# Moving the minimum-and-add of the Q features from VectorE to GpSimd in a linear-attention and MLP block

## Chip, cores and metric

The kernel runs on one core of a Trainium2 chip. The metric is the device time of one execution in microseconds (us). Medians and ratios here are of fast runs, or of samples in which a rare slow run does not move the median.

## The reference

Two branches share one layer-normalised input `xn` of 2048 tokens by 640 features, and their sum is added to `x`. The branch that matters here is linear attention with 32 heads of 20 features:

```python
qkv = (x @ wqkv) ...                                  # q, k, v
phi = lambda t: jnp.where(t > 0, t + 1, jnp.exp(t)) + 1e-6
pq, pk = phi(q), phi(k)
kv  = einsum("bhsd,bhse->bhde", pk, v);  z = einsum("bhsd->bhd", pk)
num = einsum("bhqd,bhde->bhqe", pq, kv)
den = einsum("bhqd,bhd->bhq", pq, z)[..., None] + 1e-6
o   = num / den  ...  @ wo
# result: x + attention(xn) + (gelu(xn @ w1 + b1) @ w2 + b2)
```

Inputs and outputs are bf16.

## The kernel before

The feature map `phi` is computed as `max(t, 0) + (min(exp(t), 1) + 1e-6)` in three instructions on two engines. ScalarE takes the exponential out of PSUM (where this kernel's matmuls put their results) into one of three buffers `ek` in SBUF (where its other tiles lie), VectorE applies minimum and add in place, and VectorE adds the maximum, again out of PSUM. Code and edits are shown cut in this document (`...`), and remarks after # are added here:

```python
def phi(src, b, nb, dst, res_dst, extra_w):           # v = "vector"
    s = ring_e[0] % 3                                  # one of three ek buffers
    ...
    Pl.ins("scalar", lambda e: e.activation(e2, src, ACT.Exp), reads=br, writes=[r_ek[s]])
    Pl.ins(v, lambda e: e.tensor_scalar(et, et, 1.0, 1e-6, ALU.min, ALU.add),
           reads=[r_ek[s]], writes=[r_ek[s]])
    Pl.ins(v, lambda e: e.scalar_tensor_tensor(out=d2, in0=src, scalar=0.0, in1=e2,
                                               op0=ALU.max, op1=ALU.add),
           reads=br + [r_ek[s]], writes=[res_dst] + extra_w)
```

The Q stage has four chunks of 512 tokens. Each chunk has five units of five 128x512 matmuls, one PSUM bank per unit, and a `phi` per unit. Between the chunks stand two other small stages:

```python
def q_chunk(c):
    for j in range(DT):                                # five units
        b = take(1)                                    # next of 8 PSUM banks, in a ring
        ...                                            # five matmuls into bank b
        phi(bank(b), b, 1, PQ[:, j, cc], r_PQ[c][j], [])

q_chunk(0)
kvt_step()        # five masked products, VectorE takes them out of PSUM
q_chunk(1)
q_chunk(2)
m_step()          # KV times Wo: five pairs of banks, ScalarE takes them out
q_chunk(3)
...
bs = [out_w2(0)]  # 24 matmuls of the MLP's second layer
db = den_step()   # denominators: needs every unit of Q
```

In these traces an engine takes up its work in program order: in the changed kernel, for example, TensorE's units of chunk 3 start at 139.67 us, behind the KV-Wo pairs that had to wait. A wait on a semaphore therefore holds everything behind it on the same engine, and the ring of eight banks lets TensorE run ahead only until it meets a bank that has not been emptied.

## Time and profile before

The median was 210.53 us (three runs, 210.5 to 210.66). The profiled execution has a span of 208.6 us.

| Reading | Value | View |
|---|---|---|
| TensorE busy | 98% of the span | busy table |
| VectorE, ScalarE, GpSimd busy | 52%, 36%, 11% | busy table |
| One Q unit on TensorE | about 1.09 us | timeline |
| Min/add, max/add of a Q unit on VectorE | 0.29, 0.69 us | timeline |
| Pause of TensorE's weight loads in the KV-Wo step | 0.42 us | timeline |

The page of before. Its busy table gives, for each engine, busy us, share of the span and number of instructions (PE is TensorE's matmuls, PEld its weight loads, DVE VectorE, ACT ScalarE, POOL GpSimd):

```profile
PE 204.4 (98%) x1599; PEld 140.6 (67%) x1599; DVE 108.1 (52%) x226; ACT 74.9 (36%) x142; POOL 22.9 (11%) x62
...
PE 92%; DVE 4%; DMA 3%; issue 0%; ACTq 0%; DVEq 0%
```

The last line is from the same page's chain of waits: the chain that ended last, followed back from the end, by engine. TensorE makes up 92% of it.

The timeline of before, from the first weight load of Q over the end of chunk 2 to the first of the denominators, gives start, length, engine, line, operation and tiles; brackets name what ended an idle time. L463 is the exponential, L464 the min/add, L466 the max/add, L551 the KV-Wo step, L526 the Q units and L561 the denominators:

```profile
104.12 5.22 PEld L526 LDWEIGHTS ps<-xnT,Wqkv 128*128 128x128 bf16 x25
...
121.12 0.60 ACT L463 ACTIVATE ek<-ps 128x512 bf16<-128x512 f32 x1 [0.48 <-PE ps L526]
121.75 0.30 DVE L464 TENSOR_SCALAR ek<-ek 128x512 bf16<-128x512 bf16 x1
122.10 1.52 PEld L551 LDWEIGHTS ps<-Wo,W 128*32 128x32 bf16 x48 [0.40 <-issue]
...
122.15 0.69 DVE L466 SCALAR_TENSOR_TENSOR PQ<-ps,ek 128x512 bf16<-128x512 f32 x1
122.20 0.60 ACT L463 ACTIVATE ek<-ps 128x512 bf16<-128x512 f32 x1 [0.48 <-PE ps L526]
122.83 0.29 DVE L464 TENSOR_SCALAR ek<-ek 128x512 bf16<-128x512 bf16 x1
...
123.23 0.69 DVE L466 SCALAR_TENSOR_TENSOR PQ<-ps,ek 128x512 bf16<-128x512 f32 x1
124.04 1.01 PEld L551 LDWEIGHTS ps<-Wo,W 128*32 128x32 bf16 x32 [0.42 <-ACT Msb L556]
...
134.07 0.77 PEld L561 LDWEIGHTS ps<-PQ,ZB 128*32 128x32 bf16 x20 [0.26 <-issue]
```

Two things are to be seen. Each min/add starts 0.03 us after its exponential ends, so VectorE, which is fully occupied here (0.29 + 0.69 us and two gaps in 1.08 us), is not behind. And the weight loads pause 0.42 us after 48 of 80, until the max/add of the last unit of chunk 2 has emptied its bank at 123.92. The bracket puts this down to ScalarE; the max/add's end, 0.12 us before the loads resume, and the chain of waits name the true releaser.

The trace has no large two-operation arithmetic on GpSimd. What it does have, by groups of one shape (busy us, then mean ns of one), is this:

```profile
L314 POOL TENSOR_SCALAR stats<-stats 128x1 f32<-128x1 f32 x16 | 3.5, 222 | 7.2 <-DVE stats L311 7.2
...
L277 POOL TENSOR_SCALAR_AFFINE_SELECT E<-E 128x512 bf16<-128x512 bf16 x1 | 0.6, 634 | 0.1
```

### The profile page before, as it was taken

Reading aid. Unit: us, or ns where it says so; the run is one execution under the profiler, and the core shown is the slowest. Engines: PE = TensorE matmul, PEld = TensorE weight load, DVE = VectorE, ACT = ScalarE, POOL = GpSimd, SP = SyncE. Lnnn points to the kernel's source line nnn. Section 1 sums busy time; section 2 is a strip of 40 time slices with the busy share of each in tenths; the row PEclk is TensorE's granted clock in tenths of the full one; section 3 lists DMA queues with packets and bytes.
Section 4 is the critical chain, followed back from the end, with each engine's and each line's share of the span. In section 5 each row is a group of like instructions: output and inputs, shape, how many; then the busy total and the mean of one; then the engine's idle time right before and its main releaser. Section 6 shows DMA issues by size and latency. Waiting matters only on the chain.

```text
span 208.6 us, 3973 instructions
## 1 busy us (share of the span) xinstructions
PE 204.4 (98%) x1599; PEld 140.6 (67%) x1599; DVE 108.1 (52%) x226; ACT 74.9 (36%) x142; POOL 22.9 (11%) x62
## 2 busy tenths in 40 slices
PE   7999999999999999999999999999999999999995
PEld 2789987444457777777756565577777777777775
DVE  4589970000007888998258965478633422523322
ACT  2689887666676455111153577100000000000000
POOL 3235568300031000000000000000000000000000
PEclk9999999999999999999999999999999999999999
DMA  5998668998000000000000000691110111001001
GB/s 172 348 351 103 104 127 120 376 332 274 3 0 0 0 3 0 0 3 0 0 3 2 0 3 0 198 312 54 63 60 31 61 42 52 31 31 35 31 35 61
DMA packets 22507, 17.86 MB, mean 86 GB/s; under 512 B 9176, under 2 KB 22488, under 8 KB 22488
## 3 DMA queue, kind: packets, MB, share of 16 engines
q1 hardware_dynamic: 21808, 17.11, 28.6%
q10 hardware_dynamic: 680, 0.49, 0.8%
q8 instruction: 12, 0.20, 0.4%
q14 instruction: 7, 0.06, 0.1%
HBM read 12.62 MB, written 2.62 MB: 73 GB/s over the span
## 4 chain that ended last, share of the span: by engine, by line
PE 92%; DVE 4%; DMA 3%; issue 0%; ACTq 0%; DVEq 0%
PE ps L622 33%; PE ps L355 25%; PE ps L514 10%; PE ps L476 10%; PE ps L526 7%; DVE PQ L466 3%; DMA W<-in_B_w_dram 3%; PE ps L658 2%; DVE ek L464 1%; PE ps L535 1%; PE ps L551 1%; PE ps L561 1%; PE ps L385 0%; PE ps L339 0%; ACTq L234 0%
## 5 line engine op out<-in xcount | busy, mean ns | idle before, releaser
L355 PE MATMUL ps<-xnT,W 128*128 128x128 bf16 (+2 forms) x435 | 52.0, 282 | 0.0
L622 PE MATMUL ps<-W,HG 128*128 128x320 bf16 x360 | 51.4, 299 | 0.0
L355 PEld LDWEIGHTS ps<-xnT,W 128*128 128x128 bf16 x435 | 35.5, 98 | 15.8 <-DMA W<-in_B_w_dram 0.2
L622 PEld LDWEIGHTS ps<-W,HG 128*128 128x128 bf16 x360 | 35.1, 98 | 14.2 <-issue 0.4
L359 ACT ACTIVATE HG<-ps,b1c 128x128 bf16<-128x128 f32 (+2 forms) x87 | 40.0, 492 | 12.7 <-PE ps L355 10.6
L464 DVE TENSOR_SCALAR ek<-ek 128x512 bf16<-128x512 bf16 (+1 forms) x36 | 11.1, 307 | 41.7 <-ACT ek L463 40.5
L641 DVE TENSOR_TENSOR out_sb<-ps,xnT 128x640 bf16<-128x640 f32 x15 | 12.4, 825 | 36.2 <-PE ps L622 36.0
L463 ACT ACTIVATE ek<-ps 128x512 bf16<-128x512 f32 (+1 forms) x36 | 23.2, 644 | 19.7 <-PE ps L526 10.1
L622 PE MATMUL ps<-Msb,PQ 128*128 128x320 bf16 x150 | 22.5, 299 | 0.0
L526 PE MATMUL ps<-xnT,Wqkv 128*128 128x512 bf16 x100 | 22.1, 379 | 0.0
L514 PE MATMUL ps<-xPK,xn_tm 128*128 128x320 bf16 x160 | 22.1, 299 | 0.0
L476 PE MATMUL ps<-Wqkv,xnT 128*128 128x320 bf16 x160 | 21.9, 299 | 0.0
L476 PEld LDWEIGHTS ps<-Wqkv,xnT 128*128 128x128 bf16 x160 | 15.7, 98 | 6.2
L514 PEld LDWEIGHTS ps<-xPK,xn_tm 128*128 128x128 bf16 x160 | 15.6, 98 | 6.0
L622 PEld LDWEIGHTS ps<-Msb,PQ 128*128 128x128 bf16 x150 | 14.6, 98 | 5.7
L526 PEld LDWEIGHTS ps<-xnT,Wqkv 128*128 128x128 bf16 x100 | 11.6, 118 | 9.5 <-ACT Msb L556 0.2
L311 DVE BATCH_NORM_STATS2 stats<-xPK 128x6 f32<-128x320 bf16 x32 | 13.6, 466 | 2.9 <-DMA xPK<-in_A_x_dram 2.7
L466 DVE SCALAR_TENSOR_TENSOR PQ<-ps,ek 128x512 bf16<-128x512 f32 x20 | 13.8, 692 | 2.1
L466 DVE SCALAR_TENSOR_TENSOR xPK<-ps,ek 128x640 bf16<-128x640 f32 x16 | 13.2, 825 | 1.7
L501 DVE TENSOR_TENSOR Msb<-Msb,xPK 128x640 f32<-128x640 f32 x14 | 11.6, 825 | 0.5
L518 ACT ACTIVATE W<-ps 128x640 bf16<-128x640 f32 x5 | 3.5, 703 | 18.6 <-PE ps L514 18.6
L321 POOL TENSOR_TENSOR rstd<-aggr,mhalf 128x1 f32<-128x1 f32 x16 | 9.1, 568 | 8.9 <-DVE aggr L319 8.9
(68 smaller groups left out, 93.9 us busy)
## 6 DMA issues: line engine op xcount, KB each, us to landing
xnT<-in_A_x_dram SPq DMA_DIRECT2D x4, 640.0 KB, 6.4
Wqkv<-in_A_wqkv_dram SPq DMA_DIRECT2D x3, 800.0 KB, 7.0
out_dram<-out_sb SPq DMA_DIRECT2D x15, 160.0 KB, 1.8
W<-in_B_w_dram SPq DMA_DIRECT2D x1, 1920.0 KB, 15.2
W<-in_B_w_dram SPq DMA_DIRECT2D x3, 480.0 KB, 7.4
xPK<-in_A_x_dram SPq DMA_DIRECT2D x2, 640.0 KB, 8.5
Wo<-in_A_wo_dram SPq DMA_DIRECT2D x1, 800.0 KB, 10.7
xPK<-in_A_x_dram SPq DMA_DIRECT2D x4, 160.0 KB, 4.4
```

What stands on the lines that cost most here:

```text
L311: Pl.ins(v, lambda e: e.bn_stats(stats[:, s, 6 * h:6 * h + 6], x_in[:, t, h * HW:(h + 1) * HW]), reads=[r_x[t]], writes=[r_stats[s][h]])
L355: Pl.ins("tensor", [(lambda e, k=k: e.matmul(bank(b, 0, w), W1[:, k, jb * P:(jb + 1) * P], xnT[:, k, tok], start=(k == 0), stop=(k == DT - ...
L359: Pl.ins("scalar", lambda e: e.activation(HG[:, jb, tok], bank(b, 0, w), ACT.Gelu_apprx_tanh, bias=b1c[:, jb:jb + 1]), reads=[B_[b], r_b1c ...
L463: Pl.ins("scalar", lambda e: e.activation(e2, src, ACT.Exp), reads=br, writes=[r_ek[s]])
L464: Pl.ins(v, lambda e: e.tensor_scalar(et, et, 1.0, 1e-6, ALU.min, ALU.add), reads=[r_ek[s]], writes=[r_ek[s]])
L466: Pl.ins(v, lambda e: e.scalar_tensor_tensor(out=d2, in0=src, scalar=0.0, in1=e2, op0=ALU.max, op1=ALU.add), reads=br + [r_ek[s]], writes= ...
L476: fns.append(lambda e, k=k, h=h, b=b, t=t: e.matmul(bank(b + h, 0, HW), xnT[:, k, t * P:(t + 1) * P], Wqkv[:, k, D + h * HW:D + (h + 1) * ...
L501: Pl.ins(v, lambda e, t=t: e.tensor_tensor(out=zsum, in0=zsum, in1=PK[:, t, :], op=ALU.add), reads=[r_PK[t], r_zsum], writes=[r_zsum])
L514: Pl.ins("tensor", [(lambda e, t=t, h=h, b=b, f=f: e.matmul(bank(b + h, 0, HW), xn_tm[:, t, f * P:(f + 1) * P], PK[:, t, h * HW:(h + 1) * ...
L526: Pl.ins("tensor", [(lambda e, k=k, j=j, b=b: e.matmul(bank(b), Wqkv[:, k, j:D:DT], xnT[:, k, cc], start=(k == 0), stop=(k == DT - 1))) fo ...
L622: return lambda e: e.matmul(bank(b + h, 0, HW), l, r[:, h * HW:(h + 1) * HW], start=(i == 0), stop=(i == JT + DT - 1))
L641: Pl.ins(v, lambda e: e.tensor_tensor(out=halves(out_sb[:, s, :]), in0=pair(b), in1=halves(x_res[:, t, :]), op=ALU.add), reads=B_[b:b + 2] ...
```

## The change

VectorE is the busier of the two engines and GpSimd is idle in the Q stage, so the change gives GpSimd the min/add of the twenty Q units. The K stage keeps VectorE.

```diff
-        def phi(src, b, nb, dst, res_dst, extra_w):
+        def phi(src, b, nb, dst, res_dst, extra_w, mid="vector"):
 ...
-            Pl.ins(v, lambda e: e.tensor_scalar(et, et, 1.0, 1e-6, ALU.min, ALU.add),
+            Pl.ins(mid, lambda e: e.tensor_scalar(et, et, 1.0, 1e-6, ALU.min, ALU.add),
 ...
-                phi(bank(b), b, 1, PQ[:, j, cc], r_PQ[c][j], [])
+                phi(bank(b), b, 1, PQ[:, j, cc], r_PQ[c][j], [], g)
```

## The prediction

> **What bounds the kernel now.** TensorE. The page's busy table gives PE 98% of the 208.6 us span, VectorE 52%, ScalarE 36%, GpSimd 11%. In the Q stage (104.3 to 130.9 us in the timeline) one unit of five 128x512 matmuls takes about 1.09 us. Per unit ScalarE's exponential takes 0.60 us, VectorE's min/add 0.29 us and its max/add out of PSUM 0.69 us; with the gaps VectorE repeats every 1.08 us. The chain of waits runs through these two VectorE lines from 115.7 to 123.9 us (3.7% of the span), but that mostly shows two engines with the same period: there the timeline has PE busy without a gap, and each min/add starts 0.03 us after its exponential, so VectorE has no backlog. PE's only real stall is in the step after chunk 2 (KV times Wo): its fourth output pair needs the PSUM banks of the last two Q units of chunk 2, and the weight loads pause 0.42 us (123.62 to 124.04) for the max/add that ends at 123.92.
>
> **What the change removes, adds, moves.** Twenty min/adds of 0.29 us (plus about 0.1 us gap each) leave VectorE. GpSimd, idle in this stage, gets twenty 128x512 bf16 one-input operations. The trace has no such GpSimd operation. Estimate: its affine selects take 0.34 us for 140 columns and 0.634 us for 512, so 0.79 ns per column over a fixed 0.23 us; its 128x1 add takes 0.22 us. That gives 0.65 us; a slower two-operation body could make it 0.9. The Trainium skill, "GPSIMD Engine Reference", section 4.1, calls one-input elementwise work on GpSimd roughly line-rate, which agrees with the affine selects. The trace shows about 0.08 us from VectorE to GpSimd and 0.14 us back.
>
> Contention: the max/add has one SBUF input (the other is PSUM), and the skill's "SBUF — State Buffer", section "Who interferes with whom", says such an instruction does not contend with GpSimd.
>
> **On the critical path.** The throughput gain is worth nothing: PE sets the 1.09 us. GpSimd keeps up while one operation with its gap stays under 1.08 us. The three exponential buffers need a latency of under three periods, about 3.2 us; the new one is about 2.2 us. What remains is latency: a unit's banks come free later by (0.65 + 0.2) minus (0.29 + 0.1), 0.4 to 0.7 us. This lands once in full, at the fourth pair of the KV-Wo step: the stall goes from 0.42 to about 0.9 us. The denominator step also waits for the last Q unit, but with about 1.3 us of slack (max/add ends 132.6, step starts 134.07).
>
> **Prediction.** 210.5 + 0.5 = 211.0 us, 80% range 210.6 to 213.0. Faster by over 2%: 0.01; within 2%: 0.90; slower by over 2%: 0.09.
>
> **What would show it.** GpSimd min/add 0.6 to 0.95 us; VectorE busy down by about 6 us, GpSimd up by 13 to 19 us; PE busy unchanged; the pause of weight loads at the fourth pair 0.8 to 1.1 us; no pause before the denominator step; max/add still 0.69 us.
>
> **What would make it wrong.** If the GpSimd operation takes over about 1.0 us, it sets the pace: units fall behind by the excess, times ten over chunks 1 and 2, plus five in chunk 3. At 1.35 us per unit that is 2.7 us plus added latency at the KV-Wo step, plus about 1 us at the denominator step: over 4 us, slower by over 2%.

## The result

The changed kernel took 231.66 us (median of four runs, 231.0 to 232.78) against 210.51 us of before on the same chip. The ratio is 1.1014, with a 95% interval of 1.0983 to 1.1046. Here and below, a ratio is the mean time of one kernel's fast runs over the mean of the other's of the same rounds, so it is not quite the ratio of the medians quoted.

The span grew from 208.6 to 229.3 us. The page of after: busy table, chain of waits by engine, and the two groups of the changed pair (count, busy us, mean ns, and idle time before them with its releaser):

```profile
PE 210.0 (92%) x1592; PEld 141.7 (62%) x1599; DVE 102.8 (45%) x206; ACT 75.0 (33%) x142; POOL 61.4 (27%) x82
...
PE 77%; POOL 14%; DVE 2%; issue 2%; DMA 1%; POOLq 1%; ACT 1%; SPq 0%; DVEq 0%; ACTq 0%
...
L464 POOL TENSOR_SCALAR ek<-ek 128x512 bf16<-128x512 bf16 x20 | 38.4, 1921 | 50.4 <-ACT ek L463 49.0
...
L466 DVE SCALAR_TENSOR_TENSOR PQ<-ps,ek 128x512 bf16<-128x512 f32 x20 | 13.8, 691 | 35.8 <-POOL ek L464 35.8
```

GpSimd, which was not in the chain before, now makes up 14% of it. The min/add takes 1.92 us on GpSimd, where the prediction had 0.65. The max/add is unchanged at 0.69 us, but now waits 35.8 us in total for GpSimd.

The timeline of after (cut):

```profile
104.00 5.22 PEld L526 LDWEIGHTS ps<-xnT,Wqkv 128*128 128x128 bf16 x25
...
106.10 29.94 POOL L464 TENSOR_SCALAR ek<-ek 128x512 bf16<-128x512 bf16 x15 [42.73 <-ACT ek L463]
...
125.73 0.75 PE L551 MATMUL ps<-Wo,W 128*32 128x320 bf16 x16
...
128.99 1.27 PE L551 MATMUL ps<-Wo,W 128*32 128x320 bf16 x16 [2.51 <-DVE PQ L466]
...
132.99 1.27 PE L551 MATMUL ps<-Wo,W 128*32 128x320 bf16 x16 [2.73 <-ACT Msb L556]
...
136.98 2.33 PE L551 MATMUL ps<-Wo,W 128*32 128x320 bf16 x32 [2.73 <-DVE PQ L466]
...
142.29 9.91 POOL L464 TENSOR_SCALAR ek<-ek 128x512 bf16<-128x512 bf16 x5 [6.25 <-ACT ek L463]
...
153.22 0.17 PEld L561 LDWEIGHTS ps<-PQ,ZB 128*32 128x32 bf16 x8 [3.80 <-DVE PQ L466]
153.26 2.33 PE L561 MATMUL ps<-PQ,ZB 128*32 128x512 bf16 x20 [3.49 <-DVE PQ L466]
```

GpSimd works through the fifteen units of chunks 0 to 2 back to back, 29.94 us for fifteen starts, or 2.0 us each. Then it has a hole of 6.25 us: the KV-Wo pairs wait for the last banks of chunk 2, and the units of chunk 3 stand behind those pairs in TensorE's queue. Then come the last five units, and the denominators (L561) start.

From the first weight load of Q to the first of the denominators it took 49.2 us (104.00 to 153.22) in place of 29.95 (104.12 to 134.07). The 49.2 us add up as 2.1 until GpSimd's first start, 29.9 for fifteen units, 6.25 of hole, 9.9 for five units, and 1.0 for the last max/add and its release. That is 19.3 of the 20.7 us by which the span grew; the denominators themselves took 1.07 us longer (2.33 against 1.26).

That last figure is a second effect. By stretches, the windows view gives length, busy us of PE, PEld, DVE, ACT and POOL, then the granted clock (1.00 is full speed), the DMA share and GB/s:

```profile
112.97:125.70 12.73, 10.97 (x49) 5.64 (x50) 5.50 (x11) 4.18 (x7) 12.25 (x7) 1.00 0.00 1
125.70:139.20 13.50, 5.54 (x81) 2.85 (x80) 4.15 (x6) 4.50 (x7) 9.95 (x6) 0.62 0.00 1
139.20:145.00 5.80, 5.45 (x22) 2.47 (x20) 0.68 (x1) 2.50 (x4) 2.63 (x2) 0.70 0.00 0
```

In the gaps of the KV-Wo step the granted clock falls. A pair that took 0.75 us at 125.73 takes 1.27 us from 128.99 on. In before, the same view gives 1.00 from 104.1 to 134.07.

### The profile page after: what moved, and what is told of

It reads as the page before. It is cut to its first block, busy times and chain, and to the rows that moved or that the text cites. A ratio compares the mean times of both kernels' runs of the same rounds, so it can differ in the third digit from the quotient of the medians.

```text
span 229.3 us, 3965 instructions
## 1 busy us (share of the span) xinstructions
PE 210.0 (92%) x1592; PEld 141.7 (62%) x1599; DVE 102.8 (45%) x206; ACT 75.0 (33%) x142; POOL 61.4 (27%) x82
## 4 chain that ended last, share of the span: by engine, by line
PE 77%; POOL 14%; DVE 2%; issue 2%; DMA 1%; POOLq 1%; ACT 1%; SPq 0%; DVEq 0%; ACTq 0%
PE ps L622 29%; PE ps L355 22%; POOL ek L464 14%; PE ps L514 9%; PE ps L476 9%; PE ps L658 2%; DMA xPK<-in_A_x_dram 1%; PE ps L526 1%; DVE PQ L466 1%; PE ps L551 1%; PE ps L561 1%; POOLq L692 1%; ACT ek L463 1%; DVE W L539 1%; PE ps L385 0%
## 5 line engine op out<-in xcount | busy, mean ns | idle before, releaser
L464 POOL TENSOR_SCALAR ek<-ek 128x512 bf16<-128x512 bf16 x20 | 38.4, 1921 | 50.4 <-ACT ek L463 49.0
L466 DVE SCALAR_TENSOR_TENSOR PQ<-ps,ek 128x512 bf16<-128x512 f32 x20 | 13.8, 691 | 35.8 <-POOL ek L464 35.8
L526 PE MATMUL ps<-xnT,Wqkv 128*128 128x512 bf16 x97 | 23.3, 397 | 3.7 <-DVE PQ L466 1.8
L464 DVE TENSOR_SCALAR ek<-ek 128x640 bf16<-128x640 bf16 x16 | 5.2, 324 | 33.8 <-ACT ek L463 32.6
L551 PE MATMUL ps<-Wo,W 128*32 128x320 bf16 x80 | 5.6, 436 | 8.0 <-DVE PQ L466 5.2
```

The lines of the kernel that those rows point to most:

```text
L464: Pl.ins(mid, lambda e: e.tensor_scalar(et, et, 1.0, 1e-6, ALU.min, ALU.add), reads=[r_ek[s]], writes=[r_ek[s]])
L526: Pl.ins("tensor", [(lambda e, k=k, j=j, b=b: e.matmul(bank(b), Wqkv[:, k, j:D:DT], xnT[:, k, cc], start=(k == 0), stop=(k == DT - 1))) fo ...
```

## The experiments

Theory A: GpSimd needs about 1.9 us for this operation by itself, more than TensorE's 1.09 us per unit, and so sets the pace. Its rivals: B, something beside it in the Q stage stretches a 0.65 us operation; C, three buffers are too few for the longer chain; D, the extra engine in the chain costs by itself.

### e1_bench: the operation alone

Added to the kernel before, on memory that is dead by then; fourteen forms, twice each, in this manner (each wait of GpSimd on itself is kept):

```diff
+            # sc, sd: 128x512 bf16; sf: fp32; started by the denominators
+            rep(lambda e: e.tensor_scalar(sc, sc, 1.0, 1e-6, ALU.min, ALU.add), R, W)
+            rep(lambda e: e.tensor_single_scalar(sc, sc, 1.0, ALU.min), R, W)
+            rep(lambda e: e.tensor_scalar(sc, sc, 1.0, 1e-6, ALU.mult, ALU.add), R, W)
+            ...
```

> The kernel before, with 28 GpSimd instructions (14 forms, twice each) on dead scratch memory, started when the denominators are done, so nothing waits for them and VectorE is mostly idle beside them. Theory A (GpSimd itself needs 1.92 us for this operation): the min/add on 128x512 bf16 takes about 1.9 us here too, about half at 256 columns and a quarter at 128 (plus a fixed part near 0.2 us), while the affine select stays near 0.63 us. Theory B (something in the Q stage, such as VectorE or ScalarE beside it, stretches a 0.65 us operation): it takes 0.65 to 0.9 us here. The one-operation forms tell what in it is slow: if each of the two operations costs a pass, min alone and add alone take about half, 0.9 to 1.1 us; if min is the slow one, add alone is near 0.65 and min alone near 1.9. If conversion from and to bf16 is what costs, the fp32 form is clearly faster.

Measured (one look, correct, 210.6 us). The per-line view of e1_bench gives minimum/median/maximum ns. L681 to L683 are the min/add at 512, 256 and 128 columns; L684 and L685 are minimum and add alone; L687 is multiply/add, L688 minimum/maximum; L689 is the min/add in fp32; L692 is a copy, L694 the affine select:

```profile
L681 POOL TENSOR_SCALAR xn_tm<-xn_tm x2: 1953/1975/1997, 141.0 to 143.1; 128x512 bf16<-128x512 bf16 x2
L682 POOL TENSOR_SCALAR xn_tm<-xn_tm x2: 1191/1218/1244, 145.2 to 146.4; 128x256 bf16<-128x256 bf16 x2
L683 POOL TENSOR_SCALAR xn_tm<-xn_tm x2: 681/778/876, 147.8 to 148.7; 128x128 bf16<-128x128 bf16 x2
L684 POOL TENSOR_SCALAR xn_tm<-xn_tm x2: 1487/1510/1533, 149.5 to 151.1; 128x512 bf16<-128x512 bf16 x2
L685 POOL TENSOR_SCALAR xn_tm<-xn_tm x2: 1490/1492/1495, 152.7 to 154.2; 128x512 bf16<-128x512 bf16 x2
...
L687 POOL TENSOR_SCALAR xn_tm<-xn_tm x2: 620/620/621, 159.0 to 159.7; 128x512 bf16<-128x512 bf16 x2
L688 POOL TENSOR_SCALAR xn_tm<-xn_tm x2: 614/614/614, 160.4 to 161.1; 128x512 bf16<-128x512 bf16 x2
L689 POOL TENSOR_SCALAR xn_tm<-xn_tm x2: 1985/2025/2065, 161.8 to 163.8; 128x512 f32<-128x512 f32 x2
...
L692 POOL COPY xn_tm<-xn_tm x2: 611/611/611, 173.2 to 173.9; 128x512 bf16<-128x512 bf16 x2
...
L694 POOL TENSOR_SCALAR_AFFINE_SELECT xn_tm<-xn_tm x2: 614/614/615, 177.2 to 177.8; 128x512 bf16<-128x512 bf16 x2
```

Theory A holds and B falls: the min/add takes 1.95 to 2.0 us here too, and 1.92 when written to another tile. The spans of GpSimd in a profile are rough, but the starts bear them out: those of the two min/adds lie 2.03 us apart, those of the two minimum/maximums 0.69. None of the three guesses about the cause was right. Minimum alone, add alone and multiply alone take about 1.5 us each, so it is neither the minimum nor one pass per operation; fp32 is no faster, so it is not the conversion. Two pairs, multiply/add and minimum/maximum, run at the speed of a copy, three times faster than the min/add and even 2.4 times faster than one of their own operations alone.

The run also shows GpSimd slowing VectorE, but only at times. VectorE's addition of two SBUF tiles (x plus bias) took 0.48 to 0.49 us in all 16 executions of before. Of the ten beside this measurement, three took 0.89 to 1.10 us and the other seven 0.48, among them three (at 151.89, 156.51 and 170.36 us) that lie wholly inside a GpSimd instruction which reads SBUF.

### e2_ring8: more buffers

```diff
             et = ek[:, s, 0:w]
+            r_e = r_ek[s]
+            if nb == 1:                        # Q units: eight buffers in dead memory
+                s = 4 + ring_q[0] % 8
+                ring_q[0] += 1
+                et, r_e = xn_tm[:, s, 0:w], r_xn[s]
 ...
```

> The changed kernel with eight exponential buffers in the Q stage in place of three. Theory A (GpSimd's throughput sets the pace): GpSimd still starts one min/add every 2.0 us, ScalarE merely runs further ahead, and the time stays within 1.5 us of 231.7. Theory C (the longer chain of exponential, min/add and max/add, held by three buffers, sets the pace): the units come every 1.1 to 1.3 us and the time falls to 211 to 215.

Measured: 231.63 us median of four runs, ratio 1.0998 (1.0945 to 1.1052). GpSimd still takes 1.92 us per unit and starts every 2.0 us; only the exponentials run further ahead. C falls. The page of e2_ring8 (L469 is the min/add, its buffers now in the tile `xn_tm`):

```profile
L469 POOL TENSOR_SCALAR xn_tm<-xn_tm 128x512 bf16<-128x512 bf16 x20 | 38.4, 1922 | 50.4 <-ACT xn_tm L468 49.0
```

### e3_short_op: the same chain with a short operation

```diff
-            Pl.ins(mid, lambda e: e.tensor_scalar(et, et, 1.0, 1e-6, ALU.min, ALU.add),
+            # on GpSimd only: passes everything, wrong result on purpose
+            Pl.ins(mid, (lambda e: e.tensor_scalar(et, et, 1.0, 1e-6, ALU.min, ALU.add)) if mid == "vector" else
+                   (lambda e: e.affine_select(out=et, in_=et, compare_op=ALU.is_ge, fill=0.0,
+                                              base=0, pattern=[[1, w]], channel_multiplier=0)),
```

> The changed kernel with GpSimd's min/add replaced by an affine select that passes every element (a wrong result on purpose: no minimum and no 1e-6). Same engines, same waits, same tiles, only the duration differs: 0.63 us as measured in the mask stage. Theory A: the whole loss is the duration; the time is what the prediction gave for 0.65 us, 210.8 to 211.3, and the pause of weight loads at the fourth pair of the KV-Wo step is 0.8 to 1.1 us. Rival D (the extra engine in the chain costs by itself, through its waits and hops): the time stays above 213.

Measured: 210.61 us median of six runs, before 210.28; ratio 1.0010 (0.9976 to 1.0043); the result is wrong as intended. The timeline of e3_short_op (L465 is the affine select, L553 the KV-Wo step):

```profile
122.70 0.61 POOL L465 TENSOR_SCALAR_AFFINE_SELECT ek<-ek 128x512 bf16<-128x512 bf16 x1 [0.47 <-ACT ek L463]
...
124.23 1.01 PEld L553 LDWEIGHTS ps<-Wo,W 128*32 128x32 bf16 x32 [0.78 <-ACT Msb L558]
```

All of the loss is the operation's duration; the added engine costs a pause that grows from 0.42 to 0.78 us. D falls, apart from those 0.36 us, which the time itself, with its interval of plus or minus 0.3%, doesn't resolve. The time fell just short of the 210.8 us that was expected as a minimum.

### e4_warm: keeping TensorE busy in its gaps

```diff
+        def fill(b, n):
+            Pl.ins("tensor", [lambda e: e.matmul(bank(b), warm[:, 0:P], warm[:], start=True, stop=True)] * n,
+                   reads=[r_warm], writes=[B_[b]])
 ...
+                if j > 0:
+                    fill(b, 8)           # before the last four pairs of the KV-Wo step
 ...
+            fill(b, 14)                  # before the denominators
```

> The changed kernel with dummy matmuls in the gaps of TensorE: eight of 512 columns before each of the last four pairs of the KV-Wo step and fourteen before the denominator step, in banks that are already free. The trace after shows a granted clock of 0.62 to 0.70 between 125.7 and 145 us and steps that took about twice as long as before (KV-Wo pairs four and five 2.33 against 1.2 us, first Q unit of chunk 3 1.93 against 1.05, denominators 2.33 against 1.26). If that slow clock is a part of the loss of its own, the clock stays near 1.0 in these stretches and the time falls by 2 to 3 us to about 229. If the clock is only a side effect hidden behind GpSimd, the time stays at 231.7 within 0.7.

Measured: 229.43 us median of four runs (229.35 to 229.57), ratio 1.0903 (1.0851 to 1.0955), against 1.1014 for after. The clock of the three stretches from 125.7 to 155 us is 1.00 throughout. In the timeline of e4_warm the pairs are back at their old length:

```profile
127.02 1.89 PE L544 MATMUL ps<-warm 128*128 128x512 bf16 x8 [0.51 <-DVE PQ L466]
129.02 0.75 PE L555 MATMUL ps<-Wo,W 128*32 128x320 bf16 x16
...
153.06 1.26 PE L568 MATMUL ps<-PQ,ZB 128*32 128x512 bf16 x20 [0.98 <-DVE PQ L466]
```

So some 2.2 us of the loss (231.66 to 229.43; the ratios, each to before on the same chip, differ by 1.1%, or 2.3 us) come from the slowed clock, shown by an edit that changes only what TensorE does in its gaps. By the two profiles hardly any of it was lost in the KV-Wo step itself, where GpSimd sets the pace: the denominators start only 0.2 us earlier (153.06 in place of 153.26), while they themselves are 1.07 us shorter. The page "TensorE: Matmul & The Clock Gate" of the Trainium skill, section "What's actually happening", says that a clock gate halves TensorE's rate when it has been idle. The trace of after agrees: from 129.0 to 130.3 us the granted clock was 0.51, and the pair's 0.75 us became 1.27. The page gives an idle window of about 3.4 us; here the pair at 128.99 ran slowly after a gap between matmuls of 2.51 us. But the length of one gap doesn't decide it: in e5_inter_after (below) a pair kept its 0.75 us after a gap of 2.38, and the ten matmuls after a gap of 1.25 ran slowly (3.63 us in place of 2.35). What decides it, no run here separates.

### e8_bench2: which pairs are quick

This continues the first measurement with other pairs, in the same manner.

> More forms of the operation alone on GpSimd, in the kernel before, as in the first measurement, where minimum with maximum and multiply with add took 0.61 to 0.62 us and minimum with add 1.92, and a minimum, add or multiply alone 1.5. Theory E: a few pairs have a quick routine of their own and all others take a general one. Then each pair falls into one of two groups, near 0.6 or near 1.9 us, and not in between. Rival F: the second operation decides, an add being slow after a minimum because of its kind (minimum and maximum are alike, multiply and add are alike, a mixed pair is slow); then maximum with minimum, add with multiply, add with add and multiply with multiply are all quick, and every mixed pair is slow.

Measured (one look, correct, 212.19 us). By the per-line view of e8_bench2, L681 is add/multiply, L682 multiply/multiply, L683 add/add, L684 maximum/minimum:

```profile
L681 POOL TENSOR_SCALAR xn_tm<-xn_tm x2: 620/642/665, 140.9 to 141.6; 128x512 bf16<-128x512 bf16 x2
L682 POOL TENSOR_SCALAR xn_tm<-xn_tm x2: 664/668/671, 142.4 to 143.1; 128x512 bf16<-128x512 bf16 x2
L683 POOL TENSOR_SCALAR xn_tm<-xn_tm x2: 1937/1966/1995, 143.9 to 146.0; 128x512 bf16<-128x512 bf16 x2
L684 POOL TENSOR_SCALAR xn_tm<-xn_tm x2: 2049/2104/2160, 148.0 to 150.1; 128x512 bf16<-128x512 bf16 x2
```

Maximum/add, add/maximum, multiply/minimum, minimum/multiply, minimum/minimum and subtract/multiply are slow as well (1.92 to 1.97 us). There are two groups and nothing between, as theory E has it. Rival F falls: add/add and maximum/minimum are slow although their operations are alike, and the order matters (minimum/maximum 0.61 us, maximum/minimum at least 2.05). Why these pairs are quick is not shown; that they have a routine of their own is a guess that fits.

### e6_minmax: the change with a quick pair, correct

Because the exponential is positive, a maximum with 0 changes nothing. The 1e-6 moves into VectorE's next instruction: `max(t, 1e-6) + min(exp(t), 1)` differs from `phi` by at most 1e-6.

```diff
-            Pl.ins(mid, lambda e: e.tensor_scalar(et, et, 1.0, 1e-6, ALU.min, ALU.add),
+            lim, op, low = (1e-6, ALU.add, 0.0) if mid == v else (0.0, ALU.max, 1e-6)
+            Pl.ins(mid, lambda e: e.tensor_scalar(et, et, 1.0, lim, ALU.min, op),
 ...
-            Pl.ins(v, lambda e: e.scalar_tensor_tensor(out=d2, in0=src, scalar=0.0, in1=e2,
+            Pl.ins(v, lambda e: e.scalar_tensor_tensor(out=d2, in0=src, scalar=low, in1=e2,
```

> The changed kernel with a correct result, but the second operation on GpSimd is a maximum with 0 in place of the addition of 1e-6, and the 1e-6 moves into VectorE's next instruction as the floor of its maximum. The measurement of forms gave 0.61 us for a minimum with a maximum, 1.92 for a minimum with an addition. If only the form of GpSimd's operation matters, the time is that of the affine select, 210.4 to 211.0 beside 210.3 of before on the same chip (ratio 1.000 to 1.003), with GpSimd's operation at 0.60 to 0.64 us.

Measured: correct, 210.75 us median of five runs, before 210.35; ratio 1.0014 (0.9982 to 1.0045). The per-line view of e6_minmax for the min/max (L465), and its timeline at the KV-Wo step (L552), one fence each:

```profile
L465 POOL TENSOR_SCALAR ek<-ek x20: 612/612/614, 106.0 to 131.8; 128x512 bf16<-128x512 bf16 x20
```

```profile
124.21 1.00 PEld L552 LDWEIGHTS ps<-Wo,W 128*32 128x32 bf16 x32 [0.79 <-ACT Msb L557]
```

The same move to the same engine, with one operation written in another way, is level with before within the interval (+0.14%) where the min/add lost 10%. It still gains nothing, although it takes VectorE's busy time from 108.1 to 102.6 us.

### e5_inter_before and e5_inter_after: the KV-Wo pairs spread

```diff
-        q_chunk(2)
-        m_step()
-        q_chunk(3)
+        q_chunk(2, [0])            # q_chunk and m_step now take the units or pairs to do
+        for j, (c, us) in enumerate([(2, [1, 2]), (2, [3, 4]), (3, [0, 1]), (3, [2, 3])]):
+            q_chunk(c, us)
+            m_step([j])
+        q_chunk(3, [4])
+        m_step([4])
```

> The kernel before with the five pairs of the KV-Wo step spread between the Q units of chunks 2 and 3, two Q units ahead of each pair. If the 0.42 us pause at the fourth pair is the only real stall of TensorE in this stage, it goes away and the time falls by 0.3 to 0.6 us (ratio 0.997 to 0.9985). If the VectorE stretch in the chain of waits (3.7% of the span) were a true limit, nothing changes, or it moves.

Measured: 210.95 us, before 210.35; ratio 1.0019 (0.9991 to 1.0046). A miss. The pause is gone, but two units and one pair now take 2.96 us (pair starts at 119.64 and 122.60) where 2 x 1.09 + 0.64 would be 2.82, with 0.64 the share of a pair of the block of before (five in 3.19 us, its pause included). Five such excesses of 0.14 us make 0.7 us, with the pause already counted in their favour. TensorE needed 30.5 us from the first unit to the denominators (103.95 to 134.47), against 29.8 before. The weight loads show 0.40 us idle at each change from Q units to a pair and 0.25 at each change back.

> The changed kernel with the same spreading. The trace after shows GpSimd idle for 6.25 us at the KV-Wo step, because its pairs wait for the last Q units of chunk 2 and the Q units of chunk 3 wait behind them in TensorE's queue. Theory A with this second part: the loss is twenty starts at 2.0 us plus that hole; with the hole gone, GpSimd runs from 106.1 to about 146.2 us without a break, the denominator step starts near 147 in place of 153.3, and the time falls by 5 to 7 us to 224.5 to 227. If the hole were not on the path, the time stays near 231.7.

Measured: 226.37 us median of four runs, ratio 1.0764 (1.0724 to 1.0805). The timeline of e5_inter_after:

```profile
106.43 39.91 POOL L464 TENSOR_SCALAR ek<-ek 128x512 bf16<-128x512 bf16 x20 [42.74 <-ACT ek L463]
...
129.31 0.75 PE L551 MATMUL ps<-Wo,W 128*32 128x320 bf16 x16 [2.38 <-DVE PQ L466]
131.30 3.63 PE L526 MATMUL ps<-xnT,Wqkv 128*128 128x512 bf16 x10 [1.25 <-DVE PQ L466]
...
145.28 6.24 PE L625 MATMUL ps<-W,HG 128*128 128x320 bf16 x24 [4.07 <-DVE PQ L466]
151.45 1.26 PE L561 MATMUL ps<-PQ,ZB 128*32 128x512 bf16 x20
```

The time fell by 5.3 us, inside the range, and GpSimd ran twenty units in 39.91 us without the hole. But one step of the expectation failed: the denominators started at 151.45, not near 147. The 24 matmuls ahead of them needed banks of the last Q units but one, so they began at 145.28, after 4.07 us of idle TensorE, and took 6.24 us in place of 3.42 at a granted clock of 0.53. This profile was that kernel's slowest run (227.75 us).

### e7_minmax_inter: both together

> The same form with the KV-Wo pairs spread. If TensorE is the only limit left, moving the work off VectorE gives nothing more: the same time as the kernel before with spread pairs, within 0.1%, which would be 0.3 to 0.6 us under before. If VectorE held something back, this one is faster than that.

Measured: 211.02 us, ratio 1.0041 (1.0003 to 1.0079, one run of 213.2 among them), so not under before, and level with e5_inter_before within the intervals: no sign that VectorE holds anything back.

### e9_shift_before and e9_shift_minmax: two units ahead of the block

```diff
+        q_chunk(3, [0, 1])
         m_step()
-        q_chunk(3)
+        q_chunk(3, [2, 3, 4])
```

> The kernel before with the first two Q units of chunk 3 put ahead of the whole KV-Wo step. Spreading all five pairs had removed the pause but cost more in switches between the two kinds of matmul (TensorE spent 30.5 us from the first Q unit to the denominators, against 29.8 before). This order keeps one block of pairs and as many switches as before, and gives the banks of chunk 2 two units (2.2 us) to be emptied. If the 0.42 us pause is real time, the fourth pair no longer waits, the stretch takes 29.4 us and the whole kernel 0.3 to 0.5 us less than before (ratio 0.9975 to 0.9987, inside the noise of the interval, so the trace decides). If it stays at 29.8, the pause was made up for elsewhere.

Measured: 210.2 us median of five runs, before 210.25; ratio 1.0001 (0.9989 to 1.0013). A miss that shows an error in my reasoning. The weight loads of e9_shift_before still pause:

```profile
124.59 1.52 PEld L551 LDWEIGHTS ps<-Wo,W 128*32 128x32 bf16 x48 [0.41 <-issue]
126.53 1.01 PEld L551 LDWEIGHTS ps<-Wo,W 128*32 128x32 bf16 x32 [0.42 <-ACT Msb L556]
```

Three pairs use six banks, so the fourth always meets the last two banks filled ahead of the block, whichever units those are. The weight loads of three pairs take 1.52 us and a unit needs about 1.8 us to be emptied. Moving the block moves the pause with it.

> The same order with the minimum and maximum on GpSimd. The latency that GpSimd adds (0.3 us at the fourth pair) should be hidden as well, so the time is that of the same order with VectorE, within 0.15 us, and TensorE's stretch from the first Q unit to the denominators 29.4 us too. If GpSimd's part costs something else than that latency, it stays 0.3 us or more behind.

Measured: 210.9 us median of six runs, ratio 1.0032 (1.002 to 1.0044); the pause is 0.79 us, as in e6_minmax. The distance to e9_shift_before is 0.7 us by the medians, of which the trace shows 0.36 as the longer pause (30.19 against 29.83 us from the first unit to the denominators). The remaining 0.3 us is within the spread of these runs (210.51 to 211.18) and stays open. No version beat the kernel before by more than the noise.

## Why the prediction was wrong

**The step that failed** is the estimate "That gives 0.65 us; a slower two-operation body could make it 0.9". The operation takes 1.92 us. The estimate took the slope of the affine select and a fixed part from a one-column add as the cost of any one-input operation on GpSimd. The affine select and the copy belong to a quick group at 0.61 us; the min/add does not (e1_bench, e8_bench2). In support the prediction named section 4.1 of "GPSIMD Engine Reference", which calls one-input work roughly line-rate; in the runs one-input work of one size took from 0.61 to over 1.92 us, so no one rate covers it.

**What followed was in the prediction as its own escape.** "If the GpSimd operation takes over about 1.0 us, it sets the pace" is what happened. Even its example of 1.35 us per unit was too small: the trace shows 2.0 us, 0.9 above TensorE's unit. Put into the prediction's own sum, that excess times fifteen units gives about 14 us before the latency terms (an estimate), against the 21 measured; the hole and the slowed clock of the last paragraph are not in that sum. The prediction gave slower by over 2% a chance of 0.09.

**With the size it assumed, the rest of the sum was right.** e3_short_op and e6_minmax put an operation of 0.61 us in the same place and took 210.61 and 210.75 us; the pause predicted at 0.8 to 1.1 us was 0.78 and 0.79. The added latency was a little oversized: 0.36 us by the trace, not 0.4 to 0.7.

**"The throughput gain is worth nothing"** was right. VectorE lost 5.3 us of busy time in after (108.1 to 102.8) and 5.5 in e6_minmax, and no kernel became faster. The VectorE lines in the chain of waits were no limit.

**"Contention"** was judged rightly. The Trainium skill, "SBUF — State Buffer", section "Who interferes with whom", says that a VectorE instruction with at most one SBUF input, outside the two-port modes, doesn't contend with GpSimd. The traces agree: the max/add had a median of 692 ns in before and in after. It says that one with two SBUF inputs does contend with a GpSimd instruction that reads SBUF. The trace of e1_bench shows this in part: 0.48 us became 0.89 to 1.10 in three executions, but three others, wholly inside such an instruction, kept 0.48.

**"No pause before the denominator step" and an unchanged TensorE** were wrong as a consequence. The prediction had no place for the slowed clock, to which e4_warm gives 2.2 us, nor for the hole of 6.25 us, which e5_inter_after ties to the order of the KV-Wo step with a fall of 5.3 us.

## What to carry to other kernels

Before work is moved to an engine, measure that very operation there, with the same operations in the same order and shape; on GpSimd, one pair of operations took 0.61 us and a near neighbour 1.92 us. Then compare its time per unit with the period of the engine that sets the pace: under it, the move cost about 0.4 us of latency and gained nothing, because the relieved engine was not the limit; over it, the excess came back with every unit, together with a slowed TensorE clock. When a moved operation turns out slow, look for another way to write it before giving up the move.

## What the Trainium skill lacked or had wrong

- "GPSIMD Engine Reference", section 4.1, calls one-input elementwise work roughly line-rate. On 128x512 bf16, minimum/maximum, multiply/add, add/multiply and multiply/multiply took 0.61 to 0.67 us and a copy 0.61, but nine other pairs took about 1.92 us or more and a single minimum, add or multiply about 1.5 us. The page has no such list.
- The same section calls two-input operations about twice as slow as on VectorE and one-input ones roughly line-rate. In e1_bench a two-input add of 128x512 bf16 took 1.15 to 1.28 us, less than the one-input add of a constant at 1.49.
- "TensorE: Matmul & The Clock Gate", section "What's actually happening", gives an idle window of about 3.4 us. Here TensorE ran slowly with no gap between its matmuls that long: after 2.51 us in after (1.27 in place of 0.75 us per pair), and after 1.25 us in e5_inter_after, where a gap of 2.38 us had just passed without that.
